# New places for 279 instructions in a hand-ordered attention and MLP kernel, and two tile loads in order

## The chip, the cores and the metric

The kernel runs on one core of a Trainium2 chip. The metric is the device time of one execution in microseconds (us); of several runs the median counts. Besides the times there is one profiled execution of the kernel, taken by the hardware profiler, with the start and the duration of each instruction. The engines are called TensorE (PE, with its weight loads PEld), VectorE (DVE), ScalarE (ACT), GpSimd (POOL) and SyncE (SP, which here issues the DMAs).

## What is computed

x has 2048 tokens of width 576, one batch. After a layer norm without scale, a sliding attention and a Mish MLP run on the same normalised input and are added to x.

```python
def _A_ref(x, wqkv, wo):                     # 32 heads of 18, W = 8 keys, every second token back
    qkv = (x @ wqkv).reshape(B, S, 3, H, Dh)  # q, k, v
    idx = pos[:, None] - (jnp.arange(W) * 2)[None, :]
    logits = jnp.einsum("bhsd,bhswd->bhsw", q, kg) * scale   # masked where idx < 0
    o = jnp.einsum("bhsw,bhswd->bhsd", softmax(logits), vg)
    return o.reshape(B, S, D) @ wo
def _B_ref(x, w1, b1, w2):                   # 576 -> 4608 -> 576
    h = x @ w1 + b1
    return (h * jnp.tanh(softplus(h))) @ w2
xn = _layernorm(x)
return x + _A_ref(xn, wqkv, wo) + _B_ref(xn, w1, b1, w2)
```

## The kernel before

All matrix products are made in f32 accuracy from two rounded parts, a high and a low, of each operand: three matmuls take the place of one. High parts are cast by ScalarE, low parts are a subtraction on VectorE or GpSimd. The large products are cut in blocks with seven block products in place of eight, so sums and differences of blocks come ahead of them and joins of the results behind them.

Tokens run in two halves of 1024 (`hf` 0 and 1). The 4608 hidden columns are 36 tiles, taken in 18 pairs `q`. Of the first half, the second MLP product of the last six pairs is held back. It is done later as three groups (`e` = -44, -43, -42) of seven products each, at 459 to 543 us: PE L1091 into `pd`, from units `ud`, added by L1096. In this same stretch the second half's tokens come in: `x_load b n` (L122) loads tile n, `norm1 n` (L156) normalises it on ScalarE, `rem_step` (L207, L209) prepares its last columns on GpSimd, and TensorE transposes it (L92, L93, L95). The second half then has nine groups `e` = 0 to 8 of seven products (PE L1107 into `po`, from units `u`, added by L1113). Between their products stand the matmuls of the first MLP product (L833, L839), whose results go through VectorE's add (L889) and ScalarE's Mish (L890), or are copied first by ScalarE's `take` (L878). The attention runs on VectorE and GpSimd beside all this: products of q with the keys (`pr`, L706), reductions (L711, L750), products with the values (`pv`, L744). Its loads and stores are DMAs issued by SP (L646, L655, L752). At the end come the output projection's splits (`o_split`, L1151 to L1184), its matmuls (L1237), and the joins of the groups' accumulators (`p_join`, L1116).

The order of instructions on every engine is written by hand and kept: a list of some 2,600 positions (`timeline`) is emitted from front to back, and on each engine instructions run in the order of emission. A planned product stands at its plan item times 6 plus 4; each other step has a position that it would have by itself, to which the table `MOVE` adds a number. Near the stretches of this document a position is about half a microsecond (a plan item of six positions is one product of about 3 us).

```python
    def put(pos, fn, key):
        pos += MOVE.get(key, 0)
        assert pos > now[0], key
        timeline[pos].append(fn)
```

The keys name a step and its numbers: `u_sum e k qq` (L1001) forms the block sum for group e, product k and pair half qq, `u_high` (L1007) casts its high part, `u_low` (L1014) subtracts the low part, `p_fetch e k` (L1032, L1035) loads the product's weights. `att n` is the n-th step of the attention, `mish hf_b_f` a Mish with its add. Two more lists, `ON_VECTOR` and `ON_GPSIMD`, choose the engine of a step by its key. Buffers come from small rings (`xn` has 6, `w2` 4, the PSUM tags 4 each), and an instruction that needs a ring's buffer before it is free waits, with all that stands behind it on its queue.

At the start (L1280 to L1300) the x tiles 0 and 1 and five pieces of wqkv are loaded in turn; `hold` loads x tiles 2 and 3 behind a wait for the first tile's statistics, then the next pieces of wqkv and the remaining x tiles.

Of the kernel before, what the change touches and what calls it, by code (L numbers as in the profile page):

```python
# [14 lines left out]
S, D, F = 2048, 576, 4608  # L15
# [33 lines left out]
def block_kernel(ctx: ExitStack, tc: tile.TileContext, x, wq, wo, w1, b1, w2, mask, out):  # L49
    nc = tc.nc  # L50
    tpn = iter(range(1000))

    def engine(default, *key):
        k = " ".join(str(x) for x in key)
        return nc.vector if k in ON_VECTOR else nc.gpsimd if k in ON_GPSIMD else default

# [54 lines left out]
    mv1 = const.tile([P, TJ, 2], F32, name="mv1")  # L111
# [343 lines left out]
    zq = zqs_[1]  # L455
# [763 lines left out]
    def wo_part(p, part):  # L1219
# [12 lines left out]
        def mul(h, a, w, first, last=True, more=()):  # L1232
            seq = [(a[:, al, k], wo_t[w][:, wl, k]) for k in range(2) for al, wl in ((0, 0), (0, 1), (1, 0))]
            for k, w_ in more:
                seq += [(B[:, 2, k], w_[:, wl]) for wl in range(2)]
            for n, (l, r_) in enumerate(seq):
                nc.tensor.matmul(h, l, r_, start=first and n == 0, stop=n == len(seq) - 1, skip_group_check=True)  # L1237

        def acc(k, c, h):
            t = c_out(j // JB, c, j % JB // 2)[:, k] if hf else ts(k)[:, c * HC:(c + 1) * HC]  # L1240
            nc.vector.tensor_tensor(out=t, in0=h, in1=t, op=ALU.add)

        def send(k, c=None):
            if hf and c is not None:
                nc.sync.dma_start(ov[:, j + k, c * HC:(c + 1) * HC], c_out(j // JB, c, j % JB // 2)[:, k])
            elif hf == 0 and c is None:
                nc.sync.dma_start(ov[:, j + k, :], ts(k))
        def split(step):
            if p < NO - 1:
                o_split(p + 1, step)  # L1250
# [14 lines left out]
        else:  # L1265
# [4 lines left out]
            mul(h3, A22, "T4", False, more=((1, wo_t["D"]),))  # L1270
            acc(1, 0, h3)
            send(1)
            send(1, 0)
            split(3)
            mul(h1, S4, "B22", False, more=((0, r1),))
            acc(0, 1, h1)
            send(0)
            send(0, 1)

    rq0 = [odd.tile([P, 432], F32, tag="kv", bufs=4, name=f"rq0_{k}") for k in range(4)]  # L1280
    rq0.append(sb.tile([P, 432], F32, tag="tt", bufs=2, name="rq0_4"))
    accs = {0: load_x(0, [0], [0])}
    for k in range(2):
        nc.sync.dma_start(rq0[k], wq[0, k])
    accs[0] += load_x(0, [0], [1])
    for k in range(2, 5):
        nc.sync.dma_start(rq0[k], wq[0, k])

    def hold(ins):
        tiles = load_x(0, [0], [2, 3])  # L1290
        first = nc.cur_bb.bb.instructions[-len(tiles)]
        tc.add_manual_dep(first, ins.ins.name,
                          mybir.DependencyInfo(mybir.DependencyClass.Sync, mybir.DependencyReason.DATA),
                          reason="the other tiles' loads begin behind the first tile's")
        for k in range(4):
            load("wq", 5 + k)
        accs[0].extend(tiles + load_x(0, [1]))
        rest_loads()
# [11 lines left out]
    def rest_loads():  # L1310
        nc.sync.dma_start(b1c, b1)
        nc.sync.dma_start(mk, mask)
        for g in range(NQ):
            nc.sync.dma_start(kv_d[g][:, 0:HALO, :].rearrange("u t c -> u (t c)"), zeros)
# [37 lines left out]
    def first_cast(k, eng):  # L1352
        t = done["wq", 0, k] = new("wq", 0, k)
        nc.scalar.copy(t[:, 0, :], rq0[k])
        return lambda: eng.tensor_tensor(out=t[:, 1, :], in0=rq0[k], in1=t[:, 0, :].bitcast(F32),
                                         op=ALU.subtract)

    def prologue():
        for ns in ((0,), (1,), (2,), (3,), (4, 5), (6, 7)):
            ln_group(ns)  # L1360
        hold(ln_stats(0))
        ln_root(0)
        first_cast(0, nc.gpsimd)()
        ln_newton(0)
        ln_stats(1)
        low1 = first_cast(1, nc.gpsimd)
        ln_norm(0)
        low1()
        first_cast(2, nc.gpsimd)()
        ln_root(1)  # L1370
        ln_newton(1)
        ln_transpose(0, 0, 0)
        first_cast(3, nc.gpsimd)()
        ln_norm(1)
        first_cast(4, nc.gpsimd)()
        ln_stats(2)
# [157 lines left out]
    def spot(hf, q, i):  # L1534
        return at["s", hf, q, i]

    for q in range(NP):
# [6 lines left out]
        else:  # L1544
            ps_ = dict(raw=spot(0, q - 1, 0) - 3, sums=spot(0, q - 1, 2 if q == 2 else 0), wa=spot(0, q - 1, 1),
                       t0=spot(0, q - 1, 3), wc=spot(0, q - 1, 4), t1=spot(0, q - 1, 7))
# [84 lines left out]
    for g, (e, k, s) in enumerate(items):  # L1631
# [17 lines left out]
    for n in range(8):  # L1649
        c, k = divmod(n, 4)  # L1650
# [6 lines left out]
    for n in range(8):  # L1657
        c, k = divmod(n, 4)
# [34 lines left out]
    att = {}  # L1693
# [17 lines left out]
    for i in range(len(plan)):  # L1711
        w = [r_ for m, r_ in zip(marks, rate) if m <= i][-1:] or [0]
# [85 lines left out]
```

## Time and profile before

| what | value |
|---|---|
| runs | 1096.61, 1098.58, 1100.21 us; median 1098.58 |
| the profiled execution | 1096.24 us, of which the span is 1094.4 and 1.84 lies around it |
| granted TensorE clock | 1.00 over the whole span |
| PE busy | 1084.2 us (99%), 6414 matmuls |
| DVE busy | 954.2 us (87%) |
| ACT busy | 533.5 us (49%) |
| POOL busy | 753.2 us (69%) |
| DMA, mean | 265 GB/s, 77% of 16 engines |

A row of the timeline has the start in us, the duration in us, the engine, the line of the kernel, the operation, output<-input by the program's names, partitions x elements, and the count of instructions taken together. In brackets stands the engine's idle time before it and what released it. SPq is SP's queue of DMA issues. A matmul's end is modelled, its start is recorded.

### The profile page before, as it was taken

To read this page: it belongs to the slowest core of one execution; us is meant where nothing else is said; L and a number is where in the kernel's file an instruction comes from. 1 tells how busy PE (TensorE), PEld (TensorE's weight loads), DVE (VectorE), ACT (ScalarE), POOL (GpSimd) and SP (SyncE) were. 2 spreads that over 40 slices of the span, in tenths; PEclk is the share of its full clock that TensorE was granted. 3 is DMA by queue.
4 is the path that set the end of the run, shared out by engine and by line. 5 is a ranking of instruction groups with operands and counts; after the bars stand their busy time and mean duration, and the time that the engine had idled before them with its cause. 6 is when DMAs were issued, how large, how long until landed. Compare 5 with 4: busy or idle time off the path is not lost.

```text
span 1094.4 us, 18384 instructions
## 1 busy us (share of the span) xinstructions
PE 1084.2 (99%) x6414; PEld 994.4 (91%) x6414; DVE 954.2 (87%) x1585; ACT 533.5 (49%) x984; POOL 753.2 (69%) x590
## 2 busy tenths in 40 slices
PE   8999999999999999999999999999999999999998
PEld 7999999999999988899999888899988989989998
DVE  6956899999998978997875879999999999999876
ACT  6644655556546545863233365355345344525332
POOL 3433557876778877578456767888788787787762
PEclk9999999999999999999999999999999999999999
DMA  8699988988889899877597795757567757675872
GB/s 266 221 323 299 347 299 299 307 292 281 305 294 333 295 325 322 313 252 269 184 324 262 234 386 205 246 207 277 186 223 280 255 185 250 225 265 178 285 224 94
DMA packets 171520, 290.50 MB, mean 265 GB/s; under 512 B 32258, under 2 KB 107556, under 8 KB 171428
## 3 DMA queue, kind: packets, MB, share of 16 engines
q1 hardware_dynamic: 171428, 289.33, 77.0%
q8 instruction: 51, 0.84, 0.3%
q14 instruction: 41, 0.34, 0.1%
HBM read 179.05 MB, written 110.23 MB: 264 GB/s over the span
## 4 chain that ended last, share of the span: by engine, by line
PE 89%; DVE 8%; DMA 1%; ACT 1%; issue 1%; POOL 1%; DVEq 0%; POOLq 0%; SPq 0%; ACTq 0%
PE h L833 28%; PE po L1107 15%; PE po L955 14%; PE pq L431 8%; PE z L601 7%; PE h L839 5%; PE pd L1091 5%; PE o L1237 5%; DVE og L750 1%; DVE accP L1113 1%; DVE u L1014 1%; DVE L L711 1%; DMA acc<-in_x 1%; DVE pr L706 0%; DVE pv L744 0%
## 5 line engine op out<-in xcount | busy, mean ns | idle before, releaser
L1107 PEld LDWEIGHTS po<-pw,u 128*128 128x128 f32 x1512 | 207.3, 188 | 8.3 <-POOL u L1014 1.2
L1107 PE MATMUL po<-pw,u 128*128 128x288 f32 x1512 | 212.6, 296 | 1.3 <-POOL u L1014 0.4
L744 POOL TENSOR_TENSOR pv<-L,kv 128x576 f32<-128x576 f32 x109 | 160.1, 1569 | 48.3 <-issue 14.8
L955 PEld LDWEIGHTS po<-w,act 128*128 128x128 f32 x1152 | 157.8, 188 | 4.0
L955 PE MATMUL po<-w,act 128*128 128x288 f32 x1152 | 160.4, 295 | 0.0
L706 POOL TENSOR_TENSOR pr<-q,kv 128x576 f32<-128x576 f32 x75 | 124.5, 1676 | 12.1 <-DVE L L711 5.5
L833 PE MATMUL h<-xt,t 128*128 128x512 f32 x432 | 110.8, 392 | 0.6 <-DVE rt L889 0.6
L833 PE MATMUL h<-S,t 128*128 128x512 f32 x432 | 110.3, 390 | 0.0
L833 PE MATMUL h<-xt,wa 128*128 128x512 f32 x432 | 105.7, 393 | 0.0
L1113 DVE TENSOR_TENSOR accP<-po,accP 128x288 f32<-128x288 f32 x240 | 94.4, 445 | 4.9 <-PE po L1107 4.5
L833 PEld LDWEIGHTS h<-xt,wa 128*128 128x128 f32 x432 | 81.1, 188 | 18.4 <-POOL wa L309 0.3
L833 PEld LDWEIGHTS h<-xt,t 128*128 128x128 f32 x432 | 79.3, 188 | 16.9 <-DVE rt L889 1.3
L431 PE MATMUL pq<-wq,xt 128*128 128x432 f32 x448 | 91.6, 361 | 2.4 <-ACT xt L98 2.4
L833 PEld LDWEIGHTS h<-S,t 128*128 128x128 f32 x432 | 78.6, 188 | 13.9 <-ACT ra L878 0.2
L750 DVE TENSOR_REDUCE og<-pv 128x144 f32<-128x1152 f32 x64 | 85.7, 1341 | 5.2 <-POOL pv L744 5.0
L431 PEld LDWEIGHTS pq<-wq,xt 128*128 128x128 f32 x448 | 82.9, 188 | 7.6 <-ACT xt L98 3.4
L711 DVE TENSOR_REDUCE L<-pr 128x64 f32<-128x1152 f32 x64 | 85.7, 1342 | 1.6 <-POOL pr L706 1.0
L959 DVE TENSOR_TENSOR acc<-po,acc 128x288 f32<-128x288 f32 x192 | 76.0, 446 | 4.8 <-PE po L955 4.5
L1091 PE MATMUL pd<-pd,ud 128*128 128x288 f32 x456 | 62.6, 296 | 0.0
L1091 PEld LDWEIGHTS pd<-pd,ud 128*128 128x128 f32 x456 | 61.3, 188 | 0.4 <-DVE acc L1096 0.2
L833 PE MATMUL h<-S,wc 128*128 128x512 f32 x216 | 55.7, 393 | 0.0
L706 DVE TENSOR_TENSOR pr<-q,kv 128x576 f32<-128x576 f32 x53 | 51.7, 989 | 0.0
(337 smaller groups left out, 2239.5 us busy)
## 6 DMA issues: line engine op xcount, KB each, us to landing
kv<-kv_d SPq DMA_DIRECT2D x64, 396.0 KB, 5.4
pw<-kept_T SPq DMA_DIRECT2D x36, 576.0 KB, 4.0
kept_t<-t SPq DMA_DIRECT2D x36, 512.0 KB, 4.9
t<-kept_t SPq DMA_DIRECT2D x36, 512.0 KB, 4.7
pw<-kept_B SPq DMA_DIRECT2D x27, 576.0 KB, 5.4
rw<-in_w SPq DMA_DIRECT2D x36, 320.0 KB, 4.8
kept_B<-w SPq DMA_DIRECT2D x36, 288.0 KB, 5.0
kept_wq<-wq SPq DMA_DIRECT2D x18, 432.0 KB, 5.7
```

The lines of the kernel that those rows point to most:

```text
L431: nc.tensor.matmul(pq[:, 0:432], XT[:, xi, tok], wt[wi][:, hl, 0:432], start=i == 0, stop=i == len(seq) - 1)
L601: nc.tensor.matmul(h, l, r_, start=first and n == 0, stop=n == len(seq) - 1, skip_group_check=True)
L706: engine(nc.gpsimd, "pr", n, k, c, x).tensor_tensor(out=pr[:, x:x + hh], in0=q[:, j0 + x:j0 + x + hh, None, :].to_broadcast([P, hh, W, CU] ...
L711: nc.vector.tensor_reduce(L[:, k, j0:j0 + hj].rearrange("p j w h -> p (j w h)"), pr.rearrange("p j w (h d) -> p (j w h) d", h=2), axis=AX, ...
L744: engine(nc.gpsimd, "pv", n, k, h, x).tensor_tensor(out=pr[:, x:x + hj].rearrange("p j d w -> p j w d"), in0=L[:, k, x:x + hj, :, h:h + 1] ...
L750: nc.vector.tensor_reduce(og[:, :, c0:c0 + DH], pr, axis=AX, op=ALU.add)
L833: nc.tensor.matmul(ph, wt[:, wl, wk * P:(wk + 1) * P], X[:, xs, :], start=first and i == 0, stop=last and i == len(seq) - 1, skip_group_ch ...
L955: nc.tensor.matmul(po, acts[hf, q, b, j][:, al, tok], done["w2", hf, 2 * q + j][:, wl, c * HC:(c + 1) * HC], start=i == 0, stop=i == 5)
L959: nc.vector.tensor_tensor(out=t, in0=po, in1=t, op=ALU.add)
L1091: nc.tensor.matmul(po, units[e, k, qq][:, al, n * P:(n + 1) * P], w[qq][:, wl, :], start=i == 0, stop=i == 5)
L1107: nc.tensor.matmul(po, units[e, k, qq][:, al, tok], w[:, qq, wl, :], start=i == 0, stop=i == 5)
L1113: nc.vector.tensor_tensor(out=t, in0=po, in1=t, op=ALU.add)
```

## The change

The diff has three parts.

1. `MOVE` has 279 keys with another number. By kind: u_low 45, u_high 44, u_sum 42, act 25, att 21, p_fetch 19, mish 18, fetch 12, p_join 9, wo_fetch 7, rem_step 6, y_load 6, norm1 5, o_load 5, o_split 4, x_load b 4, exp 2, wa_high 2, wa_low 2, d_diff 1.
2. Fifteen steps change the engine. To GpSimd go `u_low -44 3 1`, `u_low -44 6 0`, `u_sum -44 3 1`, `u_low 5 1 1`, `u_low 8 1 0`, `u_sum 8 6 0`. To VectorE go `u_low -44 1 1`, `u_low -44 5 1`, half a product each of `pr 1_3 1 0 2` and `pr 1_4 1 1 2`, `u_sum 4 0 0`, `u_low 8 0 1`, `u_sum 8 5 0`, `p_join P4 P7 1`, `p_join P5 P7 0`.
3. The loads of x tiles 2 and 3 are issued in order with the others, without the wait, and so ahead of wq 5; `hold` is gone, and what else it loaded is issued at the end of the prologue, in the same order on SP.

The positions that matter here, before and after:

| step | before | after |
|---|---|---|
| u_sum -44 6 0 (GpSimd) | 1185 | 1191 |
| rem_step 4, second half (GpSimd) | 1189 | 1189 |
| u_sum -43 0 1 (VectorE) | 1186 | 1215 |
| u_low -44 3 1 (to GpSimd) | 1183 | 1190 |
| u_low -44 6 0 (to GpSimd) | 1212 | 1239 |
| x_load b 4 | 1153 | 1108 |
| x_load b 2, b 3 | 1111, 1123 | same |
| norm1 3 | 1159 | 1167 |
| mish 1_0_20 | 2017 | 2035 |
| take of c22 (ScalarE) | 2020 | 2020 |
| att 101, att 102 | 2036, 2048 | 2045, 2048 |
| u_low 4 0 1 | 2052 | 2054 |
| p_fetch 4 0 | 1994 | 2040 |
| u_sum 8 6 0 (to GpSimd) | 2530 | 2530 |
| o_split 1 | 2536 | 2537 |
| u_high 8 6 1, u_low 8 6 1 | 2535, 2536 | 2537, 2537 |

The diff, with the table cut to three of its entries, of which the first is new:

```diff
-MOVE = {..., "u_sum -43 0 1": -27, "p_fetch 4 0": -23, ...}
+MOVE = {..., "x_load b 4": -45, "u_sum -43 0 1": 2, "p_fetch 4 0": 23, ...}
...
-    accs = {0: load_x(0, [0], [0])}
-    for k in range(2):
-        nc.sync.dma_start(rq0[k], wq[0, k])
+    accs = {0: []}
+    accs[0] += load_x(0, [0], [0])
+    nc.sync.dma_start(rq0[0], wq[0, 0])
+    nc.sync.dma_start(rq0[1], wq[0, 1])
     accs[0] += load_x(0, [0], [1])
-    for k in range(2, 5):
-        nc.sync.dma_start(rq0[k], wq[0, k])
-
-    def hold(ins):
-        tiles = load_x(0, [0], [2, 3])
-        first = nc.cur_bb.bb.instructions[-len(tiles)]
-        tc.add_manual_dep(first, ins.ins.name,
-                          mybir.DependencyInfo(mybir.DependencyClass.Sync, mybir.DependencyReason.DATA),
-                          reason="the other tiles' loads begin behind the first tile's")
+    nc.sync.dma_start(rq0[2], wq[0, 2])
+    nc.sync.dma_start(rq0[3], wq[0, 3])
+    nc.sync.dma_start(rq0[4], wq[0, 4])
+    accs[0] += load_x(0, [0], [2])
+    accs[0] += load_x(0, [0], [3])
+
+    def other_loads():
         for k in range(4):
             load("wq", 5 + k)
-        accs[0].extend(tiles + load_x(0, [1]))
+        accs[0].extend(load_x(0, [1]))
         rest_loads()
...
-        hold(ln_stats(0))
+        ln_stats(0)
...
         first_cast(4, nc.gpsimd)()
+        other_loads()
         ln_stats(2)
```

## Rows read from the trace of the kernel before

**Rows 1.** The page's part on busy time: each engine's share and instructions.

```profile
PE 1084.2 (99%) x6414; PEld 994.4 (91%) x6414; DVE 954.2 (87%) x1585; ACT 533.5 (49%) x984; POOL 753.2 (69%) x590
```

**Rows 2.** Busy us by stretch; columns: stretch, us, PE, PEld, DVE, ACT, POOL, PEclk, DMA, GB/s.

```profile
455.00:491.00 36.00, 35.05 (x252) 33.05 (x251) 34.66 (x62) 26.53 (x56) 24.04 (x27) 1.00 0.83 284
770.00:930.00 160.00, 159.18 (x942) 143.92 (x941) 153.41 (x231) 71.39 (x112) 130.14 (x88) 1.00 0.65 230
```

**Rows 3.** The chain of waits: start, us, engine, line, matmuls; one product.

```profile
648.07 3.17 PE po L1107 x24
```

**Rows 4.** Timeline, SP's issues and VectorE at the start: start us, us, engine, line.

```profile
5.02 1.06 SPq L74 DMA_DIRECT2D acc<-in_x  x2
...
10.99 0.82 DVE L129 BATCH_NORM_STATS2 st<-acc 128x6 f32<-128x288 f32 x2
```

**Rows 5.** Timeline of TensorE, 471 to 477 us, held-back pairs.

```profile
471.02 0.27 PE L93 MATMUL tb<-ident,xn 128*128 128x128 f32 x1
471.62 0.33 PE L95 MATMUL tb<-ident,rem 128*128 128x128 f32 x1 [0.33 <-POOL rem L209]
...
475.43 0.27 PE L93 MATMUL tb<-ident,xn 128*128 128x128 f32 x1
475.54 0.27 PE L95 MATMUL tb<-ident,rem 128*128 128x128 f32 x1
476.40 0.66 PE L1091 MATMUL pd<-pdwb,ud 128*128 128x288 f32 x3 [0.60 <-DVE acc L1096]
```

**Rows 6.** Timeline of GpSimd and VectorE in the same stretch.

```profile
468.98 1.73 POOL L1001 TENSOR_TENSOR rd_w<-rd_w,rd_w 128x512 f32<-128x512 f32 x1
...
470.51 0.75 DVE L1001 TENSOR_TENSOR rd_w<-rd_w,rd_w 128x512 f32<-128x512 f32 x1
```

**Rows 7.** Timelines of SP, TensorE, ScalarE near 455; last row from the DMA issues.

```profile
453.26 1.29 SPq L122 DMA_DIRECT2D xn<-in_x  x1
...
454.59 0.60 PE L92 MATMUL tt<-ident,xn 128*128 128x128 f32 x4
...
461.03 0.87 ACT L156 ACTIVATE xn<-xn,nm,rs 128x576 f32<-128x576 f32 x1
...
xn<-in_x SPq DMA_DIRECT2D x4, 288.0 KB, 5.3
```

**Rows 8.** Timeline, all engines, 811 to 815 us, middle groups.

```profile
811.25 3.33 PE L1107 MATMUL po<-pw,u 128*128 128x288 f32 x24
...
812.92 0.72 ACT L890 ACTIVATE ra<-ra,b1c 128x512 f32<-128x512 f32 x1 [1.91 <-DVE ra L889]
...
814.15 0.69 DVE L889 TENSOR_TENSOR rt<-h,rt 128x512 f32<-128x512 f32 x1 [1.26 <-ACT rt L878]
...
814.89 1.66 PE L833 MATMUL h<-xt,t 128*128 128x512 f32 x6 [0.32 <-DVE rt L889]
```

**Rows 9.** Timelines of VectorE and TensorE, 818 to 827 us.

```profile
818.91 1.34 DVE L711 TENSOR_REDUCE L<-pr 128x64 f32<-128x1152 f32 x1
...
820.17 0.74 DVE L706 TENSOR_TENSOR pr<-q,kv 128x576 f32<-128x576 f32 x1
...
826.05 0.68 DVE L1014 TENSOR_TENSOR u<-rm,u 128x512 fp32r<-128x512 f32 x1
...
826.63 3.33 PE L1107 MATMUL po<-pw,u 128*128 128x288 f32 x24
```

**Rows 10.** Timeline of GpSimd and VectorE at 783.8 us.

```profile
783.77 1.43 POOL L706 TENSOR_TENSOR pr<-q,kv 128x576 f32<-128x576 f32 x1
783.83 1.92 DVE L1014 TENSOR_TENSOR u<-ra,u 128x512 fp32r<-128x512 f32 x1
```

**Rows 11.** Timeline, all engines, 1024 to 1027 us, last group.

```profile
1024.93 0.38 PE L1169 MATMUL ot<-ident,o 128*128 128x128 f32 x2
...
1025.37 1.29 POOL L1014 TENSOR_TENSOR u<-rm,u 128x512 fp32r<-128x512 f32 x1 [4.40 <-PE ot L1169]
...
1025.70 3.83 PE L1107 MATMUL po<-pw,u 128*128 128x288 f32 x24 [0.39 <-ACT u L1007]
```

More of the change, by code (lines that the diff above doesn't have):

```diff
@@ L45 @@
-ON_GPSIMD = ("d_low w B21", "d_low w B22", "d_low w T1", "low t0 11", "low t0 14", "low t0 9", "low t1 12", "low t1 13", "low t1 2", "low t1 5", "low w2 0", "low w2 10", "low w2 12", "low w2 13", "low w2 14", "low w2 15", "low w2 16", "low w2 18", "low w2 2", "low w2 20", "low w2 23", "low w2 6", "low w2 8", "low wa 0", "low wa 11", "low wa 15", "low wa 16", "low wa 3", "low wa 5", "low wa 7", "low wc 10", "low wc 11", "low wc 12", "low wc 15", "low wc 2", "low wc 3", "low wc 4", "low wc 8", "low wc 9", "low wq 10", "low wq 11", "low wq 18", "low wq 6", "low wq 7", "s_low 0 0 0", "s_low 0 0 1", "s_low 0 1 2", "s_low 0 1 3", "s_low 1 0 0", "s_low 1 0 2", "s_low 1 0 3", "s_low 1 1 1", "s_low 1 1 2", "s_low 1 1 3", "t_low T2 0", "t_low T2 1", "t_low T2 4", "t_low T2 5", "t_low T2 6", "t_low T2 7", "t_low T2 9", "t_low T3 10", "t_low T3 3", "t_low T3 4", "t_low T3 6", "t_low T3 8", "t_low T3 9", "t_sum T3 0", "t_sum T3 1", "t_sum T3 11", "t_sum T3 2", "t_sum T3 3", "t_sum T3 7", "u_low -42 2 1", "u_low -42 3 1", "u_low -42 5 1", "u_low -42 6 0", "u_low -42 6 1", "u_low -43 0 1", "u_low -43 3 1", "u_low -43 5 1", "u_low -43 6 0", "u_low -44 0 1", "u_low -44 5 1", "u_low 0 5 1", "u_low 0 6 1", "u_low 1 0 1", "u_low 1 4 1", "u_low 1 5 1", "u_low 1 6 0", "u_low 1 6 1", "u_low 2 3 1", "u_low 2 5 1", "u_low 2 6 1", "u_low 3 3 1", "u_low 3 5 1", "u_low 3 6 0", "u_low 4 3 1", "u_low 4 6 0", "u_low 4 6 1", "u_low 5 0 1", "u_low 5 3 1", "u_low 5 5 1", "u_low 5 6 0", "u_low 5 6 1", "u_low 6 6 1", "u_low 7 4 1", "u_low 7 5 1", "u_low 7 6 0", "u_low 8 3 1", "u_low 8 5 1", "u_low 8 6 1", "u_sum -42 2 0", "u_sum -42 3 0", "u_sum -43 0 0", "u_sum -43 3 0", "u_sum -43 5 0", "u_sum -43 6 1", "u_sum -44 0 0", "u_sum 0 0 0", "u_sum 0 0 1", "u_sum 1 0 0", "u_sum 1 5 0", "u_sum 1 6 1", "u_sum 2 5 0", "u_sum 2 6 1", "u_sum 3 5 1", "u_sum 3 6 1", "u_sum 4 0 0", "u_sum 4 0 1", "u_sum 4 3 0", "u_sum 4 5 0", "u_sum 4 5 1", "u_sum 4 6 1", "u_sum 5 3 0", "u_sum 5 5 0", "u_sum 6 0 1", "u_sum 6 6 1", "u_sum 7 5 0", "u_sum 8 3 0", "u_sum 8 5 0", "u_sum 8 6 1", "v_low 12 2", "v_low 12 3", "v_low 13 0", "v_low 14 1", "v_low 14 3", "v_low 15 0", "v_low 15 2", "v_low 15 3", "v_low 16 1", "v_low 16 3", "v_low 17 2", "v_low 17 3", "wa_low 10", "wa_low 5", "wa_low 9")
@@ new lines @@
+ON_GPSIMD = ("d_low w B21", "d_low w B22", "d_low w T1", "low t0 11", "low t0 14", "low t0 9", "low t1 12", "low t1 13", "low t1 2", "low t1 5", "low w2 0", "low w2 10", "low w2 12", "low w2 13", "low w2 14", "low w2 15", "low w2 16", "low w2 18", "low w2 2", "low w2 20", "low w2 23", "low w2 6", "low w2 8", "low wa 0", "low wa 11", "low wa 15", "low wa 16", "low wa 3", "low wa 5", "low wa 7", "low wc 10", "low wc 11", "low wc 12", "low wc 15", "low wc 2", "low wc 3", "low wc 4", "low wc 8", "low wc 9", "low wq 10", "low wq 11", "low wq 18", "low wq 6", "low wq 7", "s_low 0 0 0", "s_low 0 0 1", "s_low 0 1 2", "s_low 0 1 3", "s_low 1 0 0", "s_low 1 0 2", "s_low 1 0 3", "s_low 1 1 1", "s_low 1 1 2", "s_low 1 1 3", "t_low T2 0", "t_low T2 1", "t_low T2 4", "t_low T2 5", "t_low T2 6", "t_low T2 7", "t_low T2 9", "t_low T3 10", "t_low T3 3", "t_low T3 4", "t_low T3 6", "t_low T3 8", "t_low T3 9", "t_sum T3 0", "t_sum T3 1", "t_sum T3 11", "t_sum T3 2", "t_sum T3 3", "t_sum T3 7", "u_low -42 2 1", "u_low -42 3 1", "u_low -42 5 1", "u_low -42 6 0", "u_low -42 6 1", "u_low -43 0 1", "u_low -43 3 1", "u_low -43 5 1", "u_low -43 6 0", "u_low -44 0 1", "u_low -44 3 1", "u_low -44 6 0", "u_low 0 5 1", "u_low 0 6 1", "u_low 1 0 1", "u_low 1 4 1", "u_low 1 5 1", "u_low 1 6 0", "u_low 1 6 1", "u_low 2 3 1", "u_low 2 5 1", "u_low 2 6 1", "u_low 3 3 1", "u_low 3 5 1", "u_low 3 6 0", "u_low 4 3 1", "u_low 4 6 0", "u_low 4 6 1", "u_low 5 0 1", "u_low 5 3 1", "u_low 5 5 1", "u_low 5 6 0", "u_low 5 6 1", "u_low 6 6 1", "u_low 7 4 1", "u_low 7 5 1", "u_low 7 6 0", "u_low 8 3 1", "u_low 8 5 1", "u_low 8 6 1", "u_sum -42 2 0", "u_sum -42 3 0", "u_sum -43 0 0", "u_sum -43 3 0", "u_sum -43 5 0", "u_sum -43 6 1", "u_sum -44 0 0", "u_sum 0 0 0", "u_sum 0 0 1", "u_sum 1 0 0", "u_sum 1 5 0", "u_sum 1 6 1", "u_sum 2 5 0", "u_sum 2 6 1", "u_sum 3 5 1", "u_sum 3 6 1", "u_sum 4 0 1", "u_sum 4 3 0", "u_sum 4 5 0", "u_sum 4 5 1", "u_sum 4 6 1", "u_sum 5 3 0", "u_sum 5 5 0", "u_sum 6 0 1", "u_sum 6 6 1", "u_sum 7 5 0", "u_sum 8 3 0", "u_sum 8 6 1", "v_low 12 2", "v_low 12 3", "v_low 13 0", "v_low 14 1", "v_low 14 3", "v_low 15 0", "v_low 15 2", "v_low 15 3", "v_low 16 1", "v_low 16 3", "v_low 17 2", "v_low 17 3", "wa_low 10", "wa_low 5", "wa_low 9", )
```

4 lines of the change are left out of this document (2 added, 2 removed).

## The prediction, made before the changed kernel ran

> **What bounds the kernel now.** I read the page's busy shares first: TensorE is busy 1084.2 of the 1094.4 us of the span [rows 1], so no more than 10.2 us of idle time can be won by any reordering, whatever it moves. The change takes no matmul away; it can only remove waits of TensorE. The second view is the busy time by stretch over the two places where most of the changed slots lie [rows 2]. TensorE idles there 36.00 − 35.05 = 0.95 us and 160.00 − 159.18 = 0.82 us. VectorE has only 1.34 us free in the first and 160.00 − 153.41 = 6.59 us free in the second; GpSimd has 12 and 30 us free, ScalarE and the DMA are far from full. So each of these stretches is TensorE's, with VectorE close behind it. The third view is the chain of waits: one product, which is 24 matmuls, stands in it with 3.17 us from start to start [rows 3]. Where the timeline shows more than that between two starts, a wait lies in between. The idle column alone shows too little, because a matmul's end is modelled, so I count from start to start.
>
> **The loads at the start.** Tiles 2 and 3 are issued on SP before the load of wq 5 instead of behind it, and the wait on VectorE's first statistics goes. That wait cost SP nothing: those statistics had ended before SP reached the tiles at 5.02 us [rows 4]. The reader of tile 2, its statistics at 10.99, has no releaser in the row: VectorE comes to it from its own earlier work, about six us after the issue [rows 4]. An issue that comes half a microsecond earlier (an SP issue takes 1.06 / 2 = 0.53 us here) therefore moves nothing. wq 5 is later by two issues, 1.1 us at most. Value 0; bounds −0.5 (one issue, if a later tile were what TensorE waits for) and +1.1.
>
> **The held-back pairs, 455 to 491 us.** Two waits of TensorE are addressed.
> - The transpose of `rem` at 471.62 waits on GpSimd's `rem` [rows 5]. In the next tile such a transpose follows its predecessor after 475.54 − 475.43 = 0.11 us, so the loss is 0.60 − 0.11 = 0.49 us. On GpSimd the subtraction of `rem` stands behind `u_sum -44 6 0`, which takes 1.73 us from 468.98 to 470.71 [rows 6]. The change puts that sum two positions behind the subtraction. The sum's reader is a unit of the group's last product, and the part built from it moves to later too. Expected: −0.49.
> - At 476.40 the next product waits for L1096, the adds that free its PSUM bank: 0.86 − 0.11 = 0.75 us lost [rows 5]. VectorE does these adds late because it is full. The change takes work of about 0.7 us out of the time ahead: `u_sum -43 0 1` (0.75 us [rows 6]) goes from position 1186 to 1215, and `u_low -44 3 1` and `u_low -44 6 0` go to GpSimd. Two lows come to VectorE in return, `1 1` and `5 1`, so VectorE gains little in the whole stretch, and what is pushed back by 15 us must still be done. I expect that of these 0.75 us some 0.3 us stay. Bounds 0 and −0.75.
>
> The balance on GpSimd is one operation more, 1.29 us for 128x512 [rows 11], against 12 us free. If it is late for a product, the price is up to one such operation, +1.29. Sum for the stretch: −0.8; bounds −1.24 and +1.29.
>
> The loads of the second half's tiles are moved here too, and each is a DMA on SP. `x_load b 4` goes 45 positions forward, ahead of `x_load b 2` and `b 3`. It then takes one of the free buffers of that ring, and `x_load b 3` has to wait for the next, the one that tile 0 leaves with its transposes, which begin at 454.59 [rows 7]. SP would stand from 453.26 to about 455.4, some 2.1 us, with two stores of T2 and the loads of one attention step queued behind it. Tile 3 then lands at about 455.4 + 5.3 = 460.7 us (issue to landing of the four loads is 5.3 [rows 7]), and its normalisation now starts at 461.03 and is itself moved back by 8 positions [rows 7]. So the cover is there, thin at 0.3 us before that move and about 4 us after it. Value 0, bounds 0 and +2.1.
>
> **The middle groups, 770 to 930 us.**
> - At 814.89 the matmuls wait for VectorE's add L889, which waits for ScalarE's copy L878, which stands on ScalarE behind a Mish [rows 8]. From 811.25 to 814.89 are 3.64 us where 3.17 suffice: 0.47 lost. The change puts that Mish (`mish 1_0_20`) from position 2017 to 2035, behind the copy at 2020. Expected −0.47. The same mechanism may give 0.2 more on a copy of weights nearby (`wa_low 10`), too small for a row.
> - Against it: half a product (`pr`, L706) of attention goes from GpSimd to VectorE twice, 0.74 us each, and the attention steps 101 and 102 now stand at 2045 and 2048, right ahead of `u_low 4 0 1` at 2054. That low ends at 826.05 + 0.68 = 826.73, and the matmuls that use its unit begin at 826.63 already [rows 9]: no slack. The reduction ahead of it is 1.34 us, the half product 0.74 [rows 9]. If half a product too many lies ahead of the low, the group's first product waits 0.7. I take +0.4, bounds 0 and +1.34 (one reduction).
> - The first fetch of the group's weights, `p_fetch 4 0`, moves back by 46 positions, about 23 us at a half us each. Its new position, 2040, lies 12 ahead of that low's 2052, so it is issued near 826 − 6 = 820, and with 5.3 us to land [rows 7] it is there at 825.3, ahead of 826.63. No cost, bound +1.0 if an attention store holds SP.
>
> Sum for the stretch: −0.1; bounds −0.67 and +1.34. Two other waits of TensorE in it (near 795 and 885) hang on operations that keep their place.
>
> **The last group and the joins.** After the transposes at 1024.93 the last product starts at 1025.70, 0.77 us later where two transposes take 0.22: 0.55 lost. It then takes 3.83 us instead of 3.33, because GpSimd's low half of the unit ends at 1026.66: 0.50 more [rows 8, 11]. The change brings `u_high 8 6 1` and `u_low 8 6 1` to one position behind the transposes (2537), and moves `u_sum 8 6 0` from VectorE (0.68 us for its size [rows 9]) to GpSimd (1.29 [rows 11]). The cast goes no earlier than before, so I take a third: −0.35; bounds −1.05 and 0. Of the joins two go from GpSimd to VectorE after the low half; nobody waits for them before the output, so 0.
>
> **The sum.** 0 − 0.8 − 0.1 − 0.35 = −1.25, rounded −1.3 us. Against the profiled execution that is 1096.24 − 1.3 = 1094.9 (its span 1094.4 and 1.84 around it). The median of the three runs of before lies 2.34 us above that execution, so a median of after is forecast at 1098.58 − 1.3 = **1097.3 us**.
>
> A rule of the Trainium skill, page "SBUF — State Buffer", section "SBUF: two separate sides", speaks against moving `pr` halves to VectorE. The trace shows first what it is about: at 783.77 GpSimd began a `pr`, VectorE began a low at 783.83, and that low took 1.92 us where the same operation takes 0.68 [rows 9, 10]; it ended 0.55 us after GpSimd's. The rule says that GpSimd and a VectorE operation with two SBUF inputs hold the shared port pair exclusively, whoever starts first, for the whole instruction. By it, each operation moved to VectorE costs up to 1.24 us more than its own time where it starts behind one of GpSimd; the trace agrees in this instance.
>
> **The rivals.**
> - *All listed waits vanish.* 0.49 + 0.75 + 0.47 + 0.55 + 0.50 = 2.76 us, so 1098.58 − 2.8 = 1095.8; if the runs of after also lie as low as the profiled execution, 1096.24 − 2.8 = 1093.4. For it speaks that each edit goes at the operation which the rows name as the releaser. Against it, VectorE has 1.34 us free in the first stretch, so the work moved there finds little room.
> - *Nothing.* Each wait that goes reappears at the next VectorE or GpSimd operation: 1098.6. For it speaks that the same rows name a different engine at each wait.
> - *Slower: VectorE becomes the bound of the middle groups.* Two half products (1.48) and `u_sum 4 0 0` (0.68) come to it, `u_low 5 1 1` (0.68) goes: +1.48 us on VectorE, out of 6.59 free [rows 2]. It decides if this lies within one product, where VectorE is full, rather than across the 160 us: 1098.58 + 1.5 = 1100.1. Each moved operation that then begins behind one of GpSimd costs 1.92 − 0.68 = 1.24 more [rows 9, 10], with three of them 1103.8. For it speaks `u_low 4 0 1` with no slack; against it, 6.59 us free.
> - *The change doesn't do what it says.* 25 of the changed slots, the lows of the second half's activations, issue no instruction, so these are no change at all. The others do move.
>
> **How the numbers follow.** Forecast 0.45, all waits vanish 0.25, nothing 0.18, slower 0.12. About 0.3%, 3.3 us, is what a measurement of this kernel can tell from no change. Below 1095.3 lie most of the second case (0.20) and a part of the first (0.10, its bounds of −1.24, −0.67 and −1.05 with a median as low as the profiled execution): faster 0.30. Above 1101.9 lie the slow case with two locked operations or more, and SP's or GpSimd's bounds of the first: slower 0.12. Same 0.58. The range runs from 1093.0 (all waits, low runs) to 1100.3 (the slow case without a lock).
>
> **What would show it.** The held-back pairs are right if the transpose of `rem` near 471 follows its neighbour after 0.11 us and L1096 no longer releases the next product; wrong if GpSimd's `rem` or a `ud` low shows there instead. The middle is right if the add L889 near 814 is no longer a releaser and `po` of group 4 starts within 0.7 us of its old place against its predecessor. The end is right if the last product takes 3.3 us instead of 3.83. A stall of SP longer than 2 us near 453 that reaches tile 3's normalisation would make the load part wrong, and more than 156 us of VectorE between 770 and 930 with TensorE waiting on L1014 there would make the slow rival right.

## The result: slower by 0.42%, and the profile after

| what | before | after |
|---|---|---|
| median of seven runs each | 1097.15 us | 1102.11 us |
| ratio after / before, 95% interval | | 1.0042 (1.0030 to 1.0054) |
| span of the profiled execution | 1094.4 us | 1100.7 us |
| mean granted TensorE clock | 1.00 | 0.997 |

The forecast was 1097.3 us, that is 1.3 us less than the three runs of before known then; the measured time lies above its range, which ended at 1100.3. By the ratio the kernel became 4.6 us slower, by the two medians 5.0. Beside the seven runs shown here the changed kernel was run again later, next to its parts: 1.0043 (1.0028 to 1.0058). Two executions far from all others, 1172.75 us of the kernel before and 2759.34 us of one variant, stand in no ratio. Page and windows of the changed kernel, answering to [rows 1, 2]; the stretches are shifted by as much as TensorE is late there:

```profile
PE 1087.5 (99%) x6414; PEld 997.4 (91%) x6414; DVE 958.3 (87%) x1588; ACT 533.9 (49%) x984; POOL 747.6 (68%) x587
...
456.00:496.00 40.00, 36.71 (x253) 34.72 (x251) 37.72 (x61) 26.81 (x56) 25.46 (x29) 0.96 0.73 250
775.00:935.00 160.00, 159.01 (x940) 143.68 (x940) 154.57 (x233) 71.78 (x112) 126.17 (x86) 1.00 0.65 228
```

The middle groups look as before (159.01 busy us of 160). The held-back pairs do not: TensorE now idles 3.3 us there, and its granted clock is 0.96 in the mean.

TensorE executes the same 6414 matmuls in both kernels, in the same order. So the two traces can be laid side by side matmul by matmul, and the difference of a matmul's two starts shows where time is lost. This ledger is worked out so from the starts of the PE rows:

| stretch (us, kernel before) | change of the difference | in the other traces with these slots |
|---|---|---|
| 0 to 20, first tiles | +1.2 | in none of these; in the last run below, with the old loads |
| 464 to 468 | +0.6 | in all eight |
| 468 to 472, `rem` | −0.55 | in all eight |
| 472 to 477 | +0.5 | in all but the sixth run |
| 477 to 484 | +3.6 | +2.1 in the four that keep the order of the sum and the engines; +0.4 to +1.3 in the others |
| 484 to 488 | −0.2 | in these four; +0.4 where the sum was moved |
| 800 to 830 | −0.7 | −0.6 near 814 in all; the rest varies, by up to +1.3 (+3.1 in the eighth run) |
| 830 to 850 | +1.0 | in all with all of these slots |
| 980 to 1031 | −0.2 | −0.2 to −0.3 in all but the eighth run, +0.8 there; −0.1 to +0.1 without these slots |
| 1036 to 1050, joins | +1.5 | in all with the joins on VectorE |

What returns in the traces is 0.6 − 0.55 + 0.5 + 2.1 − 0.2 = 2.5 us in the held-back pairs, 0.3 in the middle, −0.2 in the last group and 1.5 at the joins, 4.1 us in all. Of the other 2.2 us of this execution 1.5 and 1.2 lie in two stretches at a low clock (below), and −0.5 is scattered. Steps also arise where the instructions are the same as before: between 100 and 455 us the traces lose from 0 to 2.7 us, between 930 and 980 some gain up to 1.0, the twelfth run too, which changes nothing there. These do not return and are left out of the sum.

**The held-back pairs.** TensorE's timeline of the changed kernel, answering to [rows 5]:

```profile
472.78 0.27 PE L93 MATMUL tb<-ident,xn 128*128 128x128 f32 x1
472.89 0.27 PE L95 MATMUL tb<-ident,rem 128*128 128x128 f32 x1
...
476.74 0.33 PE L95 MATMUL tb<-ident,rem 128*128 128x128 f32 x1
478.09 0.66 PE L1091 MATMUL pd<-pdwb,ud 128*128 128x288 f32 x3 [1.02 <-DVE acc L1096]
...
481.92 0.27 PE L95 MATMUL tb<-ident,rem 128*128 128x128 f32 x1
484.08 4.95 PE L1091 MATMUL pd<-pd,ud 128*128 128x288 f32 x24 [1.89 <-issue]
```

The transpose of `rem` now follows after 0.11 us, as forecast. But the product behind the next tile starts 1.35 us after its predecessor (0.86 before), and the one after it 2.16 us after its own, a new wait of 2.16 − 0.11 = 2.05 us (in the kernel before it followed at once). The column says "issue" for it; VectorE's and GpSimd's timelines name the cause:

```profile
470.03 1.78 DVE L1014 TENSOR_TENSOR ud<-rd_w,ud 128x512 fp32r<-128x512 f32 x1
...
480.18 1.64 DVE L1014 TENSOR_TENSOR ud<-rd_a,ud 128x512 fp32r<-128x512 f32 x1
481.74 1.75 DVE L1001 TENSOR_TENSOR rd_w<-rd_w,rd_w 128x512 f32<-128x512 f32 x1
483.52 1.55 DVE L1096 TENSOR_TENSOR acc<-pd,acc 128x288 f32<-128x288 f32 x4
```

```profile
469.96 1.31 POOL L1014 TENSOR_TENSOR ud<-rd_a,ud 128x512 fp32r<-128x512 f32 x1
...
479.84 1.43 POOL L706 TENSOR_TENSOR pr<-q,kv 128x576 f32<-128x576 f32 x1
481.22 1.73 POOL L1014 TENSOR_TENSOR ud<-rd_w,ud 128x512 fp32r<-128x512 f32 x1
```

Three VectorE operations of 0.68 us take 1.6 to 1.8 us, and each begins while one of GpSimd is running and ends half a microsecond after it, as in [rows 10]. At 469.96 and 481.22 GpSimd's part is a low that the change gave to it (`u_low -44 3 1`, `u_low -44 6 0`). And the sum at 481.74 is `u_sum -43 0 1`, which the change put at position 1215, one ahead of the adds at 1216 that free the PSUM banks. They start at 483.52, and the product 0.56 us later. The first step of the stretch, +0.6 at 464 to 468, is smaller waits ahead of all this: TensorE stands 0.37 us at 466.65 for VectorE's copy L99 of the new tile. It comes with these slots (the ninth run below); no run takes it apart.

**The clock.** Windows of the changed kernel around that wait, and in its first microseconds:

```profile
482.00:484.00 2.00, 0.20 (x2) 0.00 (x0) 1.97 (x3) 1.00 (x3) 0.94 (x1) 1.00 0.95 371
484.00:488.00 4.00, 3.92 (x18) 3.95 (x19) 3.94 (x8) 2.25 (x5) 0.55 (x1) 0.57 0.47 149
...
10.00:13.00 3.00, 3.00 (x9) 2.76 (x10) 2.36 (x8) 2.12 (x5) 2.59 (x5) 0.50 1.05 403
```

After TensorE had done next to nothing for two microseconds its granted clock was 0.57, for most of the time the lower of its two levels (1.2 GHz), and it did 18 matmuls where 31, 33 and 34 lie in the same four microseconds of three traces with the same wait (the first, third and eleventh run below). That is the 1.5 us by which this wait cost 3.6 and not 2.1.

**The joins.** All engines near 1044, then the second place:

```profile
1042.78 1.29 POOL L1184 TENSOR_TENSOR oS<-s,oS 128x512 fp32r<-128x512 f32 x1
1042.91 1.77 DVE L1116 TENSOR_TENSOR accP<-accP,accP 128x576 f32<-128x576 f32 x1
...
1044.61 1.01 DVE L1241 TENSOR_TENSOR y<-o,y 128x288 f32<-128x288 f32 x2
1045.11 1.85 PE L1237 MATMUL o<-wo,oS 128*128 128x288 f32 x12 [0.65 <-DVE y L1241]
...
1054.87 0.75 DVE L1116 TENSOR_TENSOR accP<-accP,accP 128x576 f32<-128x576 f32 x1
...
1056.13 1.02 PE L1237 MATMUL o<-wo,oS 128*128 128x288 f32 x6 [0.52 <-DVE y L1241]
```

A join that VectorE took over stands ahead of the adds L1241, for which the output projection waits; it begins behind a GpSimd operation and takes 1.77 us. The second join, at 1054.87, is not held: its own 0.75 us ahead of the adds make the second wait. The steps are 0.89 and 0.67 us.

**The middle and the last group**, answering to [rows 8, 11]:

```profile
816.31 3.33 PE L1107 MATMUL po<-pw,u 128*128 128x288 f32 x24
819.48 1.53 PE L833 MATMUL h<-xt,t 128*128 128x512 f32 x6
...
848.84 2.58 POOL L744 TENSOR_TENSOR pv<-L,kv 128x576 f32<-128x576 f32 x2
850.13 1.81 DVE L309 TENSOR_TENSOR wa<-wraw,wa 128x640 fp32r<-128x640 f32 x1
852.00 0.50 PE L833 MATMUL h<-xt,wa 128*128 128x512 f32 x1 [0.34 <-DVE wa L309]
...
1029.94 0.38 PE L1169 MATMUL ot<-ident,o 128*128 128x128 f32 x2
1030.51 0.89 PE L1107 MATMUL po<-pw,u 128*128 128x288 f32 x5 [0.19 <-issue]
```

The product near 816 is followed after 3.17 us, so the 0.47 is gone. Near 850 a low of weights, `wa_low 11`, held by GpSimd's `pv`, makes a new wait of 0.5 us, 0.6 with the matmul behind it. The other 0.4 of the middle's loss come at 836.07, where a product goes on as a GpSimd low (834.72, 1.30 us) ends. At the end 0.57 us remain of 0.77.

### The profile page after: what moved, and what is told of

The parts are those of the page before. It is cut to its first block, busy times and chain, and to the rows that moved or that the text cites. A ratio compares the mean times of both kernels' runs of the same rounds, so it can differ in the third digit from the quotient of the medians.

```text
span 1100.7 us, 18381 instructions
## 1 busy us (share of the span) xinstructions
PE 1087.5 (99%) x6414; PEld 997.4 (91%) x6414; DVE 958.3 (87%) x1588; ACT 533.9 (49%) x984; POOL 747.6 (68%) x587
## 4 chain that ended last, share of the span: by engine, by line
PE 86%; DVE 6%; POOL 4%; issue 2%; DMA 1%; ACT 1%; SPq 0%; POOLq 0%; DVEq 0%; ACTq 0%
PE h L833 28%; PE po L955 14%; PE po L1107 13%; PE pq L431 8%; PE z L601 7%; PE pd L1091 6%; PE h L839 5%; PE o L1237 4%; POOL pr L706 1%; DVE accP L1113 1%; DVE u L1014 1%; DVE og L750 1%; POOL u L1014 1%; DVE L L711 1%; DMA acc<-in_x 0%
## 5 line engine op out<-in xcount | busy, mean ns | idle before, releaser
L706 POOL TENSOR_TENSOR pr<-q,kv 128x576 f32<-128x576 f32 x73 | 120.0, 1658 | 10.6 <-DVE L L711 5.5
```

What stands on the lines that cost most here:

```text
L706: engine(nc.gpsimd, "pr", n, k, c, x).tensor_tensor(out=pr[:, x:x + hh], in0=q[:, j0 + x:j0 + x + hh, None, :].to_broadcast([P, hh, W, CU] ...
```

## The experiments

Theory: the loss is VectorE's queue in front of adds or lows that TensorE waits for, in the held-back pairs and at the joins: what was put there, and how long GpSimd holds it. Rivals are named with each run. Ratios are to the kernel before, run on the same chip.

**Load order back** (in the changed kernel, the old order):

```diff
+    accs = {0: load_x(0, [0], [0])}
...
+        hold(ln_stats(0))
```

> The changed kernel with only the load order at the start put back as it was before. Theory: in the trace of the changed kernel tile 0 is cast and transposed later, TensorE runs at 0.50 of its clock from 10 to 13 us, and all that follows is 1.1 to 1.2 us late. So this kernel is 1.1 us shorter than the changed one (1102.1 - 1.1 = 1101.0), its TensorE clock is 1.00 in 10 to 13 us, and the product at 45 us starts within 0.2 us of its place in the kernel before. Rival: the late cast is chance of the DMA queues in one execution and has nothing to do with the order; then the time stays at 1102.1 within 0.4 us.

Measured 1.0028 (1.0015 to 1.0041), the changed kernel 1.0042: the interval holds the 1.1 us of the theory (1.0032) and reaches the rival's lower edge (1.0038). The trace ran at 1.00 from 10 to 13 us, but so did those of the next run and the one after, which have the new order.

**The sum behind the adds:**

```diff
-"u_sum -43 0 1": 2
+"u_sum -43 0 1": 4
```

> The changed kernel with u_sum -43 0 1 two positions later, at 1217 in place of 1215, so behind the adds L1096 of the product before and not ahead of them on VectorE. Theory: the wait of 2.05 us in front of the sixth held-back product comes from VectorE, which has that sum (1.75 us) ahead of the adds that free the PSUM bank; the adds come 1.75 us earlier, the wait shrinks to about 0.3 us and the matmuls behind it keep the full clock (1.6 us more): 3.3 us shorter than the changed kernel, about 1098.8. Rival 1: the product waits for its own weights or for the low half that ends at 481.82; then a wait of 1 us or more stays and the gain is at most 1.0. Rival 2: the fall of the clock behind the wait is independent of it; then the gain is 1.75 and the half clock stays.

Measured 1.0022 (1.0011 to 1.0033), 2.0 parts in a thousand below the changed kernel: 2.2 us of the 3.3 expected. VectorE, then TensorE, of this kernel:

```profile
479.84 1.63 DVE L1014 TENSOR_TENSOR ud<-rd_a,ud 128x512 fp32r<-128x512 f32 x1
481.51 1.55 DVE L1096 TENSOR_TENSOR acc<-pd,acc 128x288 f32<-128x288 f32 x4
...
481.58 0.27 PE L95 MATMUL tb<-ident,rem 128*128 128x128 f32 x1
482.07 3.44 PE L1091 MATMUL pd<-pd,ud 128*128 128x288 f32 x24 [0.21 <-ACT ud L1007]
```

Two positions on one sum take the wait from 2.16 to 0.49 us from start to start. The products behind it give back 0.6 us, so the stretch gains 1.1; the rest of the measured gain is the clock, or chance. So VectorE's order is the cause of this wait; weights and the low half are not (rival 1).

**Joins back on GpSimd:**

```diff
-ON_VECTOR: "p_join P4 P7 1", "p_join P5 P7 0"
```

> The changed kernel with the joins P4 P7 1 and P5 P7 0 on GpSimd again, as before. Theory: on VectorE these joins (1.77 and 0.75 us) stand ahead of the adds L1241 that free the banks of the output projection, which cost 0.91 and 0.67 us there; both waits go and the kernel is 1.5 us shorter, 1100.6. Rival: the later joins on GpSimd delay the outputs and the end of the kernel, so that the gain is under 0.5 us.

Measured 1.0030 (1.0018 to 1.0042): 1.3 us of the 1.5, with an interval that holds the rival too. In its trace both waits are gone, but TensorE loses 1.6 us at 1058.75 at another add L1241, which the changed kernel does not. So the steps of this trace show no net gain, and what made the time shorter stays open.

**The three together:**

```diff
-"u_sum -43 0 1": 2
+"u_sum -43 0 1": 4
-ON_VECTOR: "p_join P4 P7 1", "p_join P5 P7 0"
+        hold(ln_stats(0))
```

> The three edits together in the changed kernel: the load order of before, u_sum -43 0 1 behind the adds, both joins on GpSimd. Theory: the three losses are separate stretches of one TensorE queue, so they add up: 1.1 + 3.3 + 1.5 = 5.9 us shorter than the changed kernel, 1096.2, that is about 1 us shorter than the kernel before (1097.15). Rival: a wait that goes in one stretch comes back in the next, as it does where another engine is the bound; then the sum is less than two thirds of 5.9.

Measured 1.0018 (1.0007 to 1.0028), 1099.6 us: 2.6 us less than the changed kernel, not 5.9. The rival of waits that come back is nearer. In the trace the held-back pairs keep 1.4 us and the middle 0.3; the 1.1 of the loads were not there to be won.

**GpSimd's low back on VectorE**, with VectorE's order ahead of the adds untouched:

```diff
+ON_VECTOR: "u_low -44 6 0"
```

> The changed kernel with u_low -44 6 0 on VectorE again, at its new position 1239; nothing else differs, and VectorE's order up to the adds at 1216 is the same. Theory: u_sum -43 0 1 takes 1.75 us in the changed kernel, not 0.68, because it begins while GpSimd runs this low (481.22 to 482.95) and ends only after it. Without it on GpSimd the sum takes 0.7 us, the adds L1096 behind it begin about 1.05 us earlier against the low ahead of them, and TensorE's wait of 2.05 us in front of the sixth held-back product falls to about 1.0. Rival: the sum is slow of itself, or the wait is set by the weights; then it stays at 2.05 and the sum at 1.75.

VectorE and TensorE of this kernel:

```profile
480.57 1.65 DVE L1014 TENSOR_TENSOR ud<-rd_a,ud 128x512 fp32r<-128x512 f32 x1
482.14 0.68 DVE L1001 TENSOR_TENSOR rd_w<-rd_w,rd_w 128x512 f32<-128x512 f32 x1
482.85 1.55 DVE L1096 TENSOR_TENSOR acc<-pd,acc 128x288 f32<-128x288 f32 x4
...
482.33 0.27 PE L95 MATMUL tb<-ident,rem 128*128 128x128 f32 x1
483.41 3.42 PE L1091 MATMUL pd<-pd,ud 128*128 128x288 f32 x24 [0.81 <-ACT xt L103]
```

The same sum at the same place of the same queue takes 0.68 us in place of 1.75, and the wait falls from 2.16 to 1.08 us. The low itself is now late on VectorE: the last product of the group waits 4.2 us for it, up to 491.8, and TensorE falls to half clock from 491 to 496, so the one time of 1107.25 us says nothing of the first part.

**One more low on VectorE:**

```diff
-ON_GPSIMD: "u_low -44 3 1"
```

> The changed kernel with u_low -44 3 1 on VectorE again, at its new position. Theory: it is this low on GpSimd (469.96 to 471.27) behind which VectorE's u_low -44 4 0 takes 1.78 us. With it on VectorE that low takes 0.68: VectorE has an operation of 0.68 more and 1.10 less of waiting, so the adds before the fifth held-back product come 0.4 us earlier and the wait there falls from 1.24 to about 0.8. Rival: what counts is the number of operations on VectorE; then one more makes the wait 1.24 + 0.68 = 1.9.

```profile
471.31 0.68 DVE L1014 TENSOR_TENSOR ud<-rd_w,ud 128x512 fp32r<-128x512 f32 x1
...
478.03 0.29 PE L95 MATMUL tb<-ident,rem 128*128 128x128 f32 x1
478.92 0.66 PE L1091 MATMUL pd<-pdwb,ud 128*128 128x288 f32 x3 [0.60 <-DVE acc L1096]
```

VectorE has one operation more and is earlier: the low takes 0.68 in place of 1.78, the wait falls by 0.46 us, and the next one to 1.37. That the count of VectorE's operations decides is refuted. The one time, 1101.7 us, says nothing of it.

**The load order alone** (in the kernel before):

```diff
-        hold(ln_stats(0))
+    accs[0] += load_x(0, [0], [2])
+    accs[0] += load_x(0, [0], [3])
```

> The kernel before with only the load order at the start changed. Theory 1: the half clock between 10 and 13 us in the one trace of the changed kernel was chance, since two other kernels with the same load order ran there at 1.00; then this kernel takes the time of the kernel before within 0.1% (ratio 0.999 to 1.001). Theory 2: the early loads take DMA time from the pieces of wqkv that ScalarE casts first and cost on the mean; then it is 0.5 to 1.2 us slower (ratio 1.0005 to 1.0011).

Measured 0.9996 (0.9987 to 1.0005): no effect; theory 1. A kernel with the old order, the last one below, showed a clock of 0.59 from 10 to 13 us.

**Only the slots that had shortened a wait** (in the kernel before):

```diff
+MOVE: u_sum -44 6 0 (+6), mish 1_0_20 (+18), u_sum, u_high, u_low of group 8, o_split
+ON_VECTOR, ON_GPSIMD: the four changed engines of group 8
```

> The kernel before with only those slots of the change that shortened a wait in its trace: u_sum -44 6 0 at 1191, mish 1_0_20 at 2035, and the slots and engines of group 8 with o_split; the joins, the loads and all else as before. Theory: the three gains stand by themselves: 0.5 at the transpose of rem near 471, 0.6 to 0.7 near 814, 0.3 to 0.4 from 980 to 1030, in all 1.5 us, ratio about 0.9986 and in the trace no new wait of TensorE. Rival: each gain is given back at the next wait that VectorE sets (the adds near 476, the copy of weights near 850); then the ratio is 1.000 and the steps show it at those places.

Measured 1.0013 (1.0004 to 1.0023), slower than both the theory and the rival have it. The gains at 471 (0.5) and 814 (0.6) are in the trace, and more is given back: 0.75 at the adds near 477, 0.75 near 1022, and 1.7 and 1.45 near 819 and 831. At 819:

```profile
816.09 3.56 DVE L1014 TENSOR_TENSOR u<-rm,u 128x512 fp32r<-128x512 f32 x1
816.25 2.85 POOL L706 TENSOR_TENSOR pr<-q,kv 128x576 f32<-128x576 f32 x2
...
819.70 1.59 PE L1107 MATMUL po<-pw,u 128*128 128x288 f32 x10 [1.51 <-DVE u L1014]
```

A low of 0.68 us is held for 3.56, over two products of GpSimd. The same low in the kernel before, then in the kernel with the load order alone, with the same instructions around it:

```profile
816.22 0.91 DVE L1014 TENSOR_TENSOR u<-rm,u 128x512 fp32r<-128x512 f32 x1
...
817.40 2.32 DVE L1014 TENSOR_TENSOR u<-rm,u 128x512 fp32r<-128x512 f32 x1
```

The load order alone loses 1.05 us here too, so this step is not shown to be the slots' doing.

**The held-back pairs' slots alone** (in the kernel before):

```diff
+MOVE, ON_VECTOR, ON_GPSIMD: the 53 changed keys at positions 1131 to 1219
```

> The kernel before with only the 53 changed slots and engines of the held-back pairs (positions 1131 to 1219). Theory: the steps of TensorE's queue in this stretch, 0.6 - 0.5 + 0.5 + 2.1 - 0.2 = 2.5 us in the kernels with these slots, arise here alone; 2.5 us slower than before, ratio 1.0023, with the wait of about 2 us ahead of the sixth held-back product in the trace. Rival: the loss needs the other parts (loads, joins); then the ratio is under 1.001.

Measured 1.0039 (1.0026 to 1.0053), 4.3 us. The steps of its trace in this stretch are those of the changed kernel, 2.5 us, the wait 2.04. The other 1.8 of the time look like the clock, which is not shown: four of its six runs had a mean clock of 0.998 or less and took 1101.9 to 1103.4 us, the two at 1.000 took 1100.2 and 1100.8. Over all runs with this wait (the changed kernel twice, and the first, third and ninth run) 17 of 41 had such a clock; of the 93 of variants without it, 6. But within the changed kernel's own twelve runs the five at 0.999 or 1.000 took 1100.05 to 1102.38 us and the seven below 1101.81 to 1103.34, hardly less.

**The late slots alone** (in the kernel before):

```diff
+MOVE, ON_VECTOR, ON_GPSIMD: the changed keys behind position 1900
-ON_VECTOR: "p_join P4 P7 1", "p_join P5 P7 0"
```

> The changed kernel without the held-back pairs' slots, without the new load order and with the joins on GpSimd: so the slots of the middle groups and the last group alone. Theory: the steps are 0.3 in the middle (-0.6 and -0.1 near 814, +1.0 near 850) and -0.35 in the last group, together about 0: ratio 0.999 to 1.001. Rival: these stretches carry a part of the loss; then the ratio is above 1.0015.

Measured 1.0016 (1.0006 to 1.0027): the rival, though the interval reaches the theory's 1.001. Two waits are new in the trace. Near 827 a product waits 1.27 us for `u_low 4 0 1`, behind VectorE's half products. And near 1057:

```profile
1053.68 0.38 SPq L1212 DMA_DIRECT2D y<-y_d  x1
...
1056.50 0.60 PE L1151 MATMUL ot<-ident,o 128*128 128x128 f32 x4
1057.94 1.02 DVE L1241 TENSOR_TENSOR y<-o,y 128x288 f32<-128x288 f32 x2 [2.34 <-PE ot L1151]
1058.45 0.80 PE L1237 MATMUL o<-wo,oS 128*128 128x288 f32 x4 [1.35 <-DVE y L1241]
```

The add waits for y 6, which is loaded at 1053.68, behind y 7; before it was issued at 1048.81, ahead of it.

**The changed kernel again**, with no edit:

> The changed kernel itself, once more, beside the kernel before on the same chip as the parts. Theory: the steps that return in every trace are 2.5 (held-back pairs), 0.3 (middle), -0.35 (last group) and 1.55 (joins), 4.0 us in all; where TensorE's clock falls behind the wait of 2.05 or at the start, up to 2.5 more: ratio 1.0035 to 1.005. Rival: 1.0042 was partly chance of the chip; then under 1.003.

Measured 1.0043 (1.0028 to 1.0058), as the theory has it; its trace kept 1.00 at the start and behind the wait, and ends 3.9 us late.

**The joins alone** (in the kernel before):

```diff
+ON_VECTOR: "p_join P4 P7 1", "p_join P5 P7 0"
```

> The kernel before with only the joins P4 P7 1 and P5 P7 0 on VectorE, at the places of before. Theory: each stands on VectorE ahead of adds L1241 that TensorE waits for, and where it begins behind one of GpSimd it takes 1.8 us in place of 0.75: 0.7 to 0.9 us for each, 1.5 together, ratio 1.0014, with two waits of TensorE at L1237 released by VectorE's L1241. Rival: at the old places, with other joins around them on GpSimd, they fall into free time; then the ratio is 1.000 and no such wait is in the trace.

Measured 1.0008 (0.9997 to 1.0019). In the trace both joins take 1.77 us, and two waits released by L1241 step by 0.85 and 0.78, 1.5 in the net as in the changed kernel. The rival's absence of waits is refuted; the time alone would not have told.

**Late slots with the loads of y in their old order:**

```diff
+MOVE: y_load 0, 1, 4, 5, 6, 7 as before
```

> The kernel of the late slots alone (middle and last group, joins on GpSimd) with the six changed loads of y at their places of before. Theory: in the traces of two kernels with the joins on GpSimd TensorE waits 1.5 us near 1057 for the add of y 6; the change has the load of y 6 behind that of y 7, 5 us later than before. With the old places that wait goes, the kernel is 1.5 us shorter than the late slots alone (ratio 1.0016 there), so 1.000 to 1.0005. Rival: the wait comes from the outputs o or from the DMA queue as a whole and returns at another add; then the ratio stays at 1.0015.

Measured 0.9999 (0.9985 to 1.0013). The wait near 1057 is gone from the trace, y 6 is issued at 1050.66, and nothing returns at another add. The wait near 827 did not come in this trace either, so the time alone does not price the loads of y; the step does, 1.5 us.

**And the two half products back on GpSimd:**

```diff
-ON_VECTOR: "pr 1_3 1 0 2", "pr 1_4 1 1 2"
```

> As the run before, and the two half products pr 1_3 1 0 2 and pr 1_4 1 1 2 on GpSimd again. Theory: the wait of 1.27 us near 827 in the trace of the late slots comes from VectorE, which has 1.42 us of pr in one piece ahead of u_low 4 0 1; with one half on GpSimd the low ends 0.7 us earlier and that wait is 0.6 or less. Rival: GpSimd's pr then runs beside VectorE's lows and holds them, as at 783.83 in the kernel before (1.92 in place of 0.68), and the wait near 818 or 827 is 1 us or more.

Measured 0.9998 (0.9983 to 1.0012), no difference in time. In the trace the theory fails and the rival holds; two lows are held:

```profile
814.46 1.80 DVE L1014 TENSOR_TENSOR u<-rm,u 128x512 fp32r<-128x512 f32 x1
819.51 1.83 DVE L1014 TENSOR_TENSOR u<-rm,u 128x512 fp32r<-128x512 f32 x1
```

and TensorE loses 1.3 us near 829; with the halves on VectorE (the run before) it lost nothing there. The wait near 827 is therefore not the half products' alone: it comes and goes with GpSimd's timing, and which of its operations decides stays open.

The parts add up: 0.0039 (held-back pairs), 0.0008 (joins), −0.0001 (late slots with the old loads of y) and −0.0004 (load order) are 0.0042, the changed kernel's own figure. The intervals of the four are 0.0009 to 0.0014 wide to either side, so an agreement this close is in part luck.

## Why the prediction was wrong, step by step

- **What bounds the kernel** held: 99% TensorE, and all that was lost are waits of it.
- **The loads**, 0: right (0.9996). SP did stand at `x_load b 3` (idle from 454.3 to 456.6, 2.25 us where 2.1 were worked out), and none of the tiles' transposes L92 between 459 and 489 us shows a wait.
- **Held-back pairs**, −0.8 forecast, +2.5 found, above the bound of +1.29. The first term (−0.49 at `rem`) came out exactly. The second, −0.3, failed (+0.5 there and +2.1 at the next product), at the sentence that the change takes 0.7 us of work out of the time ahead of the adds: I counted durations and moved them. Two things were missed. `u_sum -43 0 1` was followed away from position 1186 and not to 1215, though the adds of the next product stand at 1216. And the lows that went to GpSimd were priced as GpSimd's time; behind each of them a VectorE operation of 0.68 us took 1.75 to 1.8. The number for that, 1.24 per operation, was in rows 10, and I used it in the middle groups only. (The sum's −0.8 also takes the 0.3 us that its own text says stay as what is won; by the text it would be −0.94.)
- **What a wait costs** was put at its length. Behind the one of 2 us TensorE fell to the lower clock in one trace of five, and the price there was 3.6 instead of 2.1.
- **Middle groups**, −0.1 forecast, +0.3 found: right in size. The 0.47 at 814 went (−0.6 with its neighbour); in the changed kernel the loss came not at `u_low 4 0 1` but at `wa_low 11`, held for 1.81 us, and at the GpSimd low near 836.
- **Last group**, −0.35 forecast, −0.2 found, at the place named, and the last product did not come down to 3.3 us, since GpSimd's low is as late as it was.
- **Joins**, 0 forecast, +1.5 found. "Nobody waits for them" was true of the joins, not of the adds queued behind them on VectorE. The load of y 6 was not costed at all; in the changed kernel the joins' waits cover it, so that joins and y together cost 1.5 and not 3.0.
- **Slots without an instruction**: 45, not 25, since 20 of the sums are of products that need none.
- **The sum** was −1.3; what returns is +4.1, and the clock adds to it in part of the runs. The slow rival had the mechanism and a chance of 0.12; it was put into the stretch where VectorE had 6.6 us free and not into the one where it had 1.3, and the range ended at its price without one held operation. The chance for a faster kernel was also set too high: of the second case most was put below 1095.3, and its own figure was 1095.8.

The rule weighed in the prediction (the Trainium skill, page "SBUF — State Buffer", section "SBUF: two separate sides") is what these traces show where one GpSimd operation stands in the way, with 0.68 becoming 1.64 to 1.83 us. It spoke against the change, but the half products were the wrong place to apply it.

No version here beats the kernel before: the lowest three lie at 0.9996 to 0.9999, with intervals that hold 1.

## What to carry to other kernels

When an instruction moves, read what stands right behind it at its new place, on its engine, and who waits for that; the same one sum cost 1.7 us by standing one position ahead of the adds, and 0.6 behind them. Moving work from VectorE to GpSimd doesn't free its duration: where VectorE's next two-input operation began during it, up to 1.2 us came back here behind one GpSimd operation, which matters most where VectorE is full. And where single executions scatter by 4 us, lay the traces side by side along the bound engine: steps that return in every trace can be read to a tenth of a microsecond, while a median tells only the sum. Steps in stretches that no edit touched show what is chance.

## What the runs showed of the hardware

- A VectorE operation was held not over one but over two whole GpSimd instructions in a row, and the end of a third (0.68 became 3.56 us at 816.09).
- The same low beside the same instructions took 0.91 us in one execution (the kernel before) and 2.32 in another (the load order alone). In both it began while a GpSimd product ran; in the first it ended before GpSimd's next product did, in the second only after it. What decides is not shown; it is one way in which executions of one kernel can differ.
- TensorE's granted clock fell behind the wait of 2 us in one trace (0.57 from 484 to 488); the traces of four more with the same wait kept 1.00. What decides is not shown.
